# Second MLP: a norm queued behind the split of the operand lS2

## The chip, the cores and the metric

The kernel runs on one core of one Trainium2 chip. The metric is the device time of one execution, in microseconds (us), as a median over runs. Engines are named as the profile names them: PE is TensorE's matmul array and PEld its weight loads, DVE is VectorE, ACT is ScalarE, POOL is GpSimd, SP is SyncE, which issues the DMAs.

## What is computed

Linear attention, then a first MLP with a leaky activation, then a second MLP with a softmax-weighted unit and a layer norm. The change lies in the second MLP:

```python
def _moe2_ref(x, w_in, w_out, g_ln):
    h = x @ w_in                                   # 4608 x 512 by 512 x 1024
    h_max = np.max(h, axis=-1, keepdims=True)
    e = np.exp(h - h_max)
    sm = e / (np.sum(e, axis=-1, keepdims=True) + 1e-09)
    solu = h * sm
    mu = np.mean(solu, axis=-1, keepdims=True)
    var = np.mean((solu - mu) ** 2, axis=-1, keepdims=True)
    ln = (solu - mu) / np.sqrt(var + 1e-06) * g_ln
    return (ln @ w_out).astype(np.float32)         # 4608 x 1024 by 1024 x 512
```

## The kernel before

Every f32 operand of a matmul is held as a high part (the value as ACT copies it to fp32r) and a low part (what is left, by a DVE subtraction); `put` writes the two. A product is then three matmuls: high by high, high by low, low by high. Both matrix products of the second MLP are made in seven block products instead of eight, by sums and differences of quarter blocks (operands A11, A12, A22, S1 to S4 on the one side, B11, B21, B22, T1 to T4 on the other).

The rows are worked off in 18 *pairs* of 128-row tiles, z = 0 and z = 1. For pair n the steps are:

- `pe_h2(n, part)`: the first product on PE, 42 matmuls of 512 columns in two PSUM banks, h2a and h2x. ACT copies partial sums aside (r1, r2, r5, line 1411), since the next product goes on in the same bank; DVE and ACT add the halves into hs_n_0 and hs_n_1.
- `norm(n, z)`: softmax unit and layer norm of one tile. It is a chain over three engines: the maximum on DVE (line 1460), exp on ACT (1461), the sum's reciprocal and the product on DVE (1450 to 1453), square on ACT (1463), a power on POOL between two small DVE steps (1456, 1457, 1465), and the last line on ACT (1466), which writes the tile el that the next step transposes. Below, "exp", "square" and "last line" of z = 0 or z = 1 are these.
- `pe_tr(n, z)`: 8 transposes on PE into two PSUM tiles tp that are used in turn, and the operands of the second product. For z = 0 ACT copies fA11 and fA12 out and writes two high parts, DVE writes the two low parts. For z = 1 the order in the code is fA22, the sum s (1524), operand A22, the difference s3 (1527), S1, s once more (1529), S2, S3, f12 (1532), S4. The tiles are named lS1, lS2, lS3 for S1 to S3, and l1 for A22 and S4.
- `pe_out(n, part)`: the second product, 84 matmuls of 256 columns in the banks oa and ox (lines 1547 to 1549), with ACT copies or1, or2, or5 (1553) and DVE additions (1567, 1575, 1577). The third of its seven products, S2 by T2, is the first that needs lS2.

The loop over n (0 to 15) interleaves these: `pe_h2(n + 1, 0)`, `pe_tr(n, 0)`, `pe_h2(n + 1, 1)`, `pe_tr(n, 1)`, `norm(n + 1, 0)`, `pe_h2(n + 1, 2)`, loads, `pe_out(n, 0)`, `norm(n + 1, 1)`, `pe_out(n, 1)`. The code's order isn't the order on the engines. A scheduler that works before the program runs puts each engine's instructions in a row, by what it reckons to be ready; on the chip each engine takes its row strictly one after the other and waits where an operand isn't there. `tc.issue_after(ins)` tells that scheduler that whatever the block traces on the engine of `ins` comes behind `ins` in the row; it adds no wait on the chip. In the loop's early turns there is extra work: up to 14 `y_late` steps, each an ACT copy and a DVE subtraction of 256 columns into a single tile yl (its next use waits until the DMA of the last one has landed), some with a DVE addition of 128x2x128 ahead. The last pairs (`end`) are ordered by hand.

A *turn* below is one value of n in this loop.

Of the kernel before, what the change touches and what calls it, by code (L numbers as in the profile page):

```python
# [12 lines left out]
AF = mybir.ActivationFunctionType  # L13
ALU = mybir.AluOpType
# [6 lines left out]
def attention_then_two_mlps(  # L21
# [32 lines left out]
    V, S, G, T = nc.vector, nc.scalar, nc.gpsimd, nc.tensor  # L54
# [51 lines left out]
    def f32(ap):  # L106
        return ap.bitcast(F32)
# [22 lines left out]
        ]  # L130

    def put(hi, lo, src, eng=V):
        S.activation(hi, src, AF.Copy)  # L133
        eng.tensor_tensor(lo, src, f32(hi), ALU.subtract)  # L134


    wps = [tc.alloc_tile_pool(name="wp0", bufs=7 + FU, side="right")]
# [1241 lines left out]
    def load_y(n):  # L1379


        i, z = divmod(n, 2)
        ys[n] = {}
        for o in STAT:
            ys[n][o] = m2["pool"].tile([P, 2, 2, P], F32R, tag=f"y{o}", bufs=1, name=f"y_{n}_{o}")
            asked = nc.sync.dma_start(out=f32(ys[n][o]), in_=y_d[i][STAT.index(o)][:, z])
        return asked
# [4 lines left out]
    def pe_h2(n, part):  # L1392
        if part == 0:
            hb[n] = [psum["h2"].tile([P, N], F32, tag=f"h2{z}", name=f"h2{z}_{n}") for z in "ax"]
            hs[n] = [gp.tile([P, F2], F32, tag="t", name=f"hs_{n}_{z}") for z in range(2)]
        (ba, bx), (ha, hb2) = hb[n][:2], hs[n]
        op = ys[n]

        def prod(t, a, b, start):
            for z in range(2):  # L1400
                ah, al = op[a][:, 0, z, :], op[a][:, 1, z, :]
                bh, bl = wi[b, z][:, 0, :], wi[b, z][:, 1, :]
                go_on = dict(skip_group_check=not start)
                T.matmul(t, ah, bh, start=start and z == 0, stop=False, **go_on)  # L1404
                T.matmul(t, ah, bl, start=False, stop=False, **go_on)  # L1405
                at_end = T.matmul(t, al, bh, start=False, stop=z == 1, **go_on)  # L1406
            return at_end

        def hold(src, z):
            r = m2["pool"].tile([P, N], F32, tag="r", bufs=3, name=f"r{z}_{n}")  # L1410
            S.activation(r, src, AF.Copy)
            return r

        if part == 0:
            prod(ba, "A11", "B11", True)
            r1 = hold(ba, 1)
            prod(bx, "A12", "B21", True)
            V.tensor_tensor(ha[:, 0:N], bx, r1, ALU.add)
            prod(ba, "S2", "T2", False)
            hb[n].append(hold(ba, 2))  # L1420
            at_end = prod(bx, "S1", "T1", True)
            hb[n].append(hold(bx, 5))
            return at_end
        elif part == 1:
            prod(ba, "S3", "T3", False)
            V.tensor_tensor(hb2[:, N:F2], ba, hb[n][3], ALU.add)
            prod(bx, "S4", "B22", False)
            V.tensor_tensor(ha[:, N:F2], bx, hb[n][2], ALU.add)
        else:
            prod(ba, "A22", "T4", False)  # L1430
            S.activation(hb2[:, 0:N], ba, AF.Copy)
# [3 lines left out]
    def norm(n, z):  # L1435
        for piece in norm_pieces(n, z):
            piece()

    def norm_pieces(n, z):
        t = 2 * n + z  # L1440
        h = hs[n][z]
        st = m2["pool"].tile([P, 8], F32, tag="st", bufs=4, name=f"st_{t}")
        nm, se, rs, su, sq, rstd = (st[:, z:z + 1] for z in range(6))
        if t == 0:
            m2["pool"].tile([P, 3 * SHIFT], F32, name="l_edge")
        e = m2["pool"].tile([P, F2], F32, tag="el", bufs=2, name=f"el_{t}")
        lns[t] = e

        def solu():
            V.tensor_scalar_add(se, se, 1e-9)  # L1450
            V.reciprocal(rs, se)
            V.scalar_tensor_tensor(e, h, rs, e, ALU.mult, ALU.mult, accum_out=su)  # L1452
            V.tensor_scalar_mul(su, su, -1.0 / F2)

        def spread():
            V.tensor_scalar(sq, sq, 1.0 / F2, 1e-6, ALU.mult, ALU.add)
            G.tensor_tensor(rstd, sq, mhalf, ALU.pow)

        return [
            lambda: V.tensor_reduce(nm, h, AX.X, ALU.max, negate=True),  # L1460
            lambda: S.activation(e, h, AF.Exp, bias=nm, accum_out=se),
            solu,
            lambda: S.activation(h, e, AF.Square, bias=su, accum_out=sq),
            spread,
            lambda: V.tensor_tensor(su, su, rstd, ALU.mult),  # L1465
            lambda: S.activation(e, e, AF.Identity, bias=su, scale=rstd),  # L1466
        ]
# [3 lines left out]
    def lt_op(n, o):  # L1471
        free = {"A22": KEPT[0], "S4": KEPT[1], "S3": KEPT[2]}
        if n == NPR - 2 and o in free:
            b, z = free[o]
            del wi[b, z]
            t = w2p["pool"].tile([P, 2, 4, P], F32R, tag=f"{b}{z}", name=f"l{o}_{n}")
        elif o in ("S1", "S2", "S3"):
            t = m2["pool"].tile([P, 2, 4, P], F32R, tag=f"l{o}", name=f"l{o}_{n}")
        else:
            y, z = divmod(("A11", "A12", "S4", "A22").index(o), 2)  # L1480
            if (n, y) not in lts:
                lts[n, y] = pair_tile(y, f"l{y}_{n}")[:, 0:4 * N].rearrange("p (z s f q) -> p z s f q", z=2, s=2, f=4)
            t = lts[n, y][:, z]
        lts[n, o] = t
        return t

    def lt_put(n, o, src):
        t = lt_op(n, o)
        put(t[:, 0], t[:, 1], src)

    lf = {}

    def turned_rows(n, z):

        ln = lns.pop(2 * n + z)
        tps = []
        for g in range(2):
            tp = psum["o"].tile([P, 4, P], F32, tag="tp", bufs=2, name=f"tp_{n}_{z}_{g}")
            for f in range(4):
                c = (4 * g + f) * P  # L1500
                T.transpose(tp[:, f, :], ln[:, c:c + P], ident)  # L1501
            tps.append(tp)
        return tps

    def pe_tr(n, z):


        tps = turned_rows(n, z)

        def copy(o, src):  # L1510
            lf[n, o] = m2["pool"].tile([P, 4, P], F32, tag=f"f{o}", bufs=1, name=f"f{o}_{n}")
            S.activation(lf[n, o], src, AF.Copy)  # L1512

        if z == 0:
            copy("A11", tps[0])
            lt_put(n, "A11", tps[0])
            copy("A12", tps[1])
            lt_put(n, "A12", tps[1])
        else:
            copy("A22", tps[1])  # L1520
            f11, f12, f22 = (lf.pop((n, o)) for o in ("A11", "A12", "A22"))
            t = gp.tile([P, 2, N], F32, tag="rn", bufs=1, name=f"fs_{n}")
            s, s3 = (t[:, y, :].rearrange("p (f q) -> p f q", f=4) for y in range(2))
            V.tensor_tensor(s, tps[0], f22, ALU.add)
            a21 = tps[0]
            lt_put(n, "A22", tps[1])
            V.tensor_tensor(s3, f11, a21, ALU.subtract)
            lt_put(n, "S1", s)
            V.tensor_tensor(s, s, f11, ALU.subtract)
            lt_put(n, "S2", s)  # L1530
            lt_put(n, "S3", s3)
            V.tensor_tensor(f12, f12, s, ALU.subtract)
            lt_put(n, "S4", f12)
# [137 lines left out]
    def store_y(asked):  # L1671
        with tc.issue_after(asked.ins):
            while y_kept:
                y_kept.pop(0)()

    for n in range(NPR - 2):
        at_end = pe_h2(n + 1, 0)
        with ExitStack() as behind:
            if n == 0:
                behind.enter_context(tc.issue_after(at_end.ins))  # L1680
            pe_tr(n, 0)
        if n:
            store_y(asked)
        if n and y_late:
            y_late.pop(0)()
        pe_h2(n + 1, 1)
        pe_tr(n, 1)
        norm(n + 1, 0)
        pe_h2(n + 1, 2)
        asked = load_y(n + 2)  # L1690
        store_y(asked)
        pe_out(n, 0)
        norm(n + 1, 1)
        if n and y_late:
            y_late.pop(0)()
        if n < NPR - 3:
            pe_out(n, 1)
    m, n = NPR - 2, NPR - 1
# [5 lines left out]
    def end():  # L1704
# [9 lines left out]
        out_prod(m - 1, ba, "S3", "T3", False)  # L1714
        V.tensor_tensor(oy[:, W:C], ba, r5, ALU.add)
        pe_tr(m, 0)
        pe_h2(n, 1)
        top0, exp0, solu0, square0, spread0, mult0, line0 = norm_pieces(n, 0)
# [123 lines left out]
```

## Time and profile before

| what | value |
|---|---|
| median of 3 runs | 1282.57 us (1281.18 to 1283.31) |
| profiled execution, first to last instruction (span) | 1282.1 us |
| PE busy | 1243.1 us, 97% |
| PEld busy | 1111.6 us, 87% |
| DVE busy | 1009.0 us, 79% |
| ACT busy | 792.1 us, 62% |
| POOL busy | 27.0 us, 2% |

The profile is of one execution, with the start of each instruction from the span's beginning. A busy PE isn't a PE at its peak: its matmuls overlap one another and their ends are modelled. The second MLP's loop runs from about 895 to 1232 us, its hand-ordered end from there to 1282 us.

### The profile page before, as it was taken

How to read it: one execution, taken by the hardware profiler on the slowest of the kernel's cores; microseconds unless marked ns; L12 is line 12 of the kernel's file. 1: busy time of each engine (PE TensorE's matmuls, PEld its weight loads, DVE VectorE, ACT ScalarE, POOL GpSimd, SP SyncE). 2: the span in 40 equal slices, each digit the busy share in tenths (PEclk: the TensorE clock that was granted, in tenths of full speed). 3: DMA queues.
4: the chain of work that ended last, by engine and by line, in shares of the span. 5: the costliest groups of instructions: out<-in, count | busy, mean ns of one | idle time of the engine just before them, and what ended most of it. 6: DMA issues, size and time to landing. Idle time of an engine off the chain costs nothing.

```text
span 1282.1 us, 22034 instructions
## 1 busy us (share of the span) xinstructions
PE 1243.1 (97%) x8443; PEld 1111.6 (87%) x8443; DVE 1009.0 (79%) x1818; ACT 792.1 (62%) x1371; POOL 27.0 (2%) x52
## 2 busy tenths in 40 slices
PE   4899999999999999999999999999999999999998
PEld 3788898898988899998998999987888888898988
DVE  7899978988867876787889888864777778686865
ACT  5776554654655665564656655544777677777774
POOL 0100000000000000000000000000000000000000
PEclk9899999999999999999999999999999999999999
DMA  9954553454426510534666457579444335333312
GB/s 254 281 168 138 143 151 105 120 175 101 140 78 198 189 34 33 214 134 174 235 230 222 191 201 262 194 240 393 134 124 145 116 131 157 114 110 110 113 59 50
DMA packets 153401, 203.83 MB, mean 159 GB/s; under 512 B 57144, under 2 KB 105296, under 8 KB 150096
## 3 DMA queue, kind: packets, MB, share of 16 engines
q1 hardware_dynamic: 152208, 201.38, 48.7%
q0 software_dynamic: 1088, 1.05, 0.5%
q8 instruction: 66, 1.08, 0.4%
q14 instruction: 39, 0.32, 0.1%
HBM read 126.37 MB, written 76.02 MB: 158 GB/s over the span
## 4 chain that ended last, share of the span: by engine, by line
PE 75%; DVE 9%; DMA 8%; ACT 5%; issue 2%; SPq 1%; POOL 0%; ACTq 0%; DVEq 0%; POOLq 0%
PE acc L471 8%; PE acc L472 8%; PE acc L473 8%; PE ga L361 4%; PE ga L362 4%; PE ga L363 4%; PE gx L361 3%; PE gx L363 3%; PE gx L362 3%; PE oa L1547 2%; PE tp L1501 2%; PE h2a L1404 2%; PE h2a L1406 2%; PE h2a L1405 2%; PE oa L1549 2%; PE oa L1548 2%
## 5 line engine op out<-in xcount | busy, mean ns | idle before, releaser
L471 PE MATMUL acc<-gg,w 128*128 128x512 f32 x576 | 226.0, 392 | 1.4 <-ACT w L212 0.9
L472 PE MATMUL acc<-gg,w 128*128 128x512 f32 x576 | 226.9, 394 | 0.0
L473 PE MATMUL acc<-gg,w 128*128 128x512 f32 x576 | 224.2, 391 | 0.0
L473 PEld LDWEIGHTS acc<-gg,w 128*128 128x128 f32 x576 | 108.1, 188 | 23.1 <-DVE w L213 0.3
L471 PEld LDWEIGHTS acc<-gg,w 128*128 128x128 f32 x576 | 108.2, 188 | 20.9 <-ACT w L212 1.0
L472 PEld LDWEIGHTS acc<-gg,w 128*128 128x128 f32 x576 | 108.2, 188 | 17.9 <-DVE gg L134 0.3
L134 DVE TENSOR_TENSOR gg<-t,gg 128x1024 fp32r<-128x1024 f32 x72 | 87.9, 1220 | 15.3 <-ACT gg L133 15.2
L133 ACT ACTIVATE gg<-t 128x1024 fp32r<-128x1024 f32 x72 | 76.6, 1064 | 27.2 <-DVE t L452 20.0
L452 DVE SCALAR_TENSOR_TENSOR t<-rn,calpha,t 128x512 f32<-128x512 f32 x120 | 84.6, 746 | 8.2 <-ACT rn L449 8.1
L449 ACT ACTIVATE rn<-t 128x1024 f32<-128x1024 f32 x60 | 63.2, 1053 | 31.7 <-DVE t L438 31.5
L134 DVE TENSOR_TENSOR l<-tp,l 128x512 fp32r<-128x512 f32 x50 | 34.2, 684 | 46.5 <-ACT l L133 46.5
L361 PE MATMUL ga<-xT,w_S 128*128 128x256 f32 x240 | 68.2, 284 | 0.3 <-ACT r L370 0.2
L363 PE MATMUL ga<-xT,w_S 128*128 128x256 f32 x240 | 67.0, 279 | 0.0
L362 PE MATMUL ga<-xT,w_S 128*128 128x256 f32 x240 | 67.0, 279 | 0.0
L370 ACT ACTIVATE r<-ga 128x512 f32<-128x512 f32 x60 | 35.7, 596 | 42.4 <-PE ga L363 42.2
L1466 ACT ACTIVATE el<-el,st 128x1024 f32<-128x1024 f32 x36 | 44.5, 1242 | 20.9 <-DVE st L1465 10.0
L389 PE MATMUL h<-xB,w_c 128*128 128x256 f32 x192 | 55.1, 289 | 1.4 <-ACT w_c L212 1.3
L391 PE MATMUL h<-xB,w_c 128*128 128x256 f32 x192 | 55.1, 288 | 1.1 <-DVE w_c L213 1.0
L390 PE MATMUL h<-xB,w_c 128*128 128x256 f32 x192 | 54.7, 285 | 0.0
L1512 ACT ACTIVATE fA<-tp 128x512 f32<-128x512 f32 x50 | 30.2, 603 | 30.1 <-PE tp L1501 30.1
L361 PEld LDWEIGHTS ga<-xT,w_S 128*128 128x128 f32 x240 | 45.1, 188 | 2.7 <-ACT r L370 1.0
L1452 DVE SCALAR_TENSOR_TENSOR el<-hs,st,el 128x1024 f32<-128x1024 f32 x36 | 46.1, 1281 | 0.6
(408 smaller groups left out, 3994.2 us busy)
## 6 DMA issues: line engine op xcount, KB each, us to landing
y_S<-y_d SPq DMA_DIRECT2D x72, 256.0 KB, 3.0
xraw<-x_d SPq DMA_DIRECT2D x16, 1024.0 KB, 4.9
y_d<-yo_S SPq DMA_DIRECT2D x32, 512.0 KB, 3.2
y_A<-y_d SPq DMA_DIRECT2D x54, 256.0 KB, 2.7
y_d<-yo_A SPq DMA_DIRECT2D x24, 512.0 KB, 3.1
p_d<-pt SPq DMA_DIRECT2D x36, 256.0 KB, 3.2
part<-p_d SPq DMA_DIRECT2D x9, 1024.0 KB, 8.5
q<-in_q_dram SPq DMA_DIRECT2D x16, 512.0 KB, 5.6
```

The source lines that it names most:

```text
L133: S.activation(hi, src, AF.Copy)
L134: eng.tensor_tensor(lo, src, f32(hi), ALU.subtract)
L361: T.matmul(bank[:, z, :], wh, x[:, 0, c, :], start=first and z == 0, stop=False, **go_on)
L362: T.matmul(bank[:, z, :], wh, x[:, 1, c, :], start=False, stop=False, **go_on)
L363: T.matmul(bank[:, z, :], wl, x[:, 0, c, :], start=False, stop=c == 1, **go_on)
L389: T.matmul(out, w[:, 0, c, :], x[:, 0, c % 2, :], start=c == 0 and h == 0, stop=False, **go_on)
L391: T.matmul(out, w[:, 1, c, :], x[:, 0, c % 2, :], start=False, stop=c == KC - 1, **go_on)
L449: S.activation(rn, t, AF.Relu, scale=-1.0)
L452: V.scalar_tensor_tensor(t[:, j, :], rn[:, j, :], calpha[:, fg + j:fg + j + 1], t[:, j, :], ALU.mult, ALU.add)
L471: T.matmul(a, wh, g[:, 0, :], start=u == 0 and f == 0, stop=False)
L472: T.matmul(a, wh, g[:, 1, :], start=False, stop=False)
L473: T.matmul(a, wl, g[:, 0, :], start=False, stop=u == NU - 1 and f == FU - 1)
```

## The change

`put` and `lt_put` return the two instructions they make, `pe_tr` keeps those of S2, and the loop traces `norm(n + 1, 1)` in a block that queues it behind both: its ACT instructions behind the high part of lS2 of pair n, its DVE instructions behind the low part.

```diff
     def put(hi, lo, src, eng=V):
-        S.activation(hi, src, AF.Copy)
-        eng.tensor_tensor(lo, src, f32(hi), ALU.subtract)
+
+        return S.activation(hi, src, AF.Copy), eng.tensor_tensor(lo, src, f32(hi), ALU.subtract)
...
         t = lt_op(n, o)
-        put(t[:, 0], t[:, 1], src)
-
-    lf = {}
+        return put(t[:, 0], t[:, 1], src)
+
+    lf, split_at = {}, {}
...
-            lt_put(n, "S2", s)
+            split_at[n] = lt_put(n, "S2", s)
...
         pe_out(n, 0)
-        norm(n + 1, 1)
+        with ExitStack() as behind:
+            for ins in split_at.pop(n):
+                behind.enter_context(tc.issue_after(ins.ins))
+            norm(n + 1, 1)
```

No instruction is added or taken away; the rows on the engines change. On ACT in turn 9, from behind or1_9 on (el_20 and el_21, st_20 and st_21 are norm(10, 0) and norm(10, 1); lS2_9, l1_9 are operands of pair 9; r1_11, r2_11 belong to pe_h2(11)), before:

```order
L1461 ACTIVATE el_21_12125,st_21_12124<-hs_10_1_11935,st_21_12124 128x1024
L133 ACTIVATE lS2_9_12022<-fs_9_12012 128x512
L1411 ACTIVATE r1_11_12188<-h2a_11_12178 128x512
L133 ACTIVATE l1_9_12014<-fA12_9_11982 128x512
L1553 ACTIVATE or2_9_12108<-oa_9_12065 128x256
L1463 ACTIVATE hs_10_0_11934,st_20_12031<-el_20_12032,st_20_12031 128x1024
L1553 ACTIVATE or5_9_12122<-ox_9_12066 128x256
L1466 ACTIVATE el_20_12032<-el_20_12032,st_20_12031 128x1024
L1463 ACTIVATE hs_10_1_11935,st_21_12124<-el_21_12125,st_21_12124 128x1024
L1580 ACTIVATE ob1_9_12068<-oa_9_12065 128x256
L1466 ACTIVATE el_21_12125<-el_21_12125,st_21_12124 128x1024
L1411 ACTIVATE r2_11_12203<-h2a_11_12178 128x512
```

The same place on ACT after the change:

```order
L134 ACTIVATE lS2_9_12022<-fs_9_12012 128x512
L134 ACTIVATE l1_9_12014<-fA12_9_11982 128x512
L1411 ACTIVATE r1_11_12188<-h2a_11_12178 128x512
L1553 ACTIVATE or2_9_12108<-oa_9_12065 128x256
L1553 ACTIVATE or5_9_12122<-ox_9_12066 128x256
L1461 ACTIVATE el_21_12125,st_21_12124<-hs_10_1_11935,st_21_12124 128x1024
L1463 ACTIVATE hs_10_0_11934,st_20_12031<-el_20_12032,st_20_12031 128x1024
L1466 ACTIVATE el_20_12032<-el_20_12032,st_20_12031 128x1024
L1463 ACTIVATE hs_10_1_11935,st_21_12124<-el_21_12125,st_21_12124 128x1024
L1580 ACTIVATE ob1_9_12068<-oa_9_12065 128x256
L1411 ACTIVATE r2_11_12203<-h2a_11_12178 128x512
L1466 ACTIVATE el_21_12125<-el_21_12125,st_21_12124 128x1024
```

The exp of z = 1 moves from the head of the piece to behind or5, five rows on; r2 moves from behind the last line of z = 1 to ahead of it.

On DVE in turn 9, from behind the low part of lS1_9 and the first small step of norm(10, 0), before:

```order
L1460 TENSOR_REDUCE st_21_12124<-hs_10_1_11935 128x1
L1529 TENSOR_TENSOR fs_9_12012<-fs_9_12012,fA11_9_11977 128x512
L134 TENSOR_TENSOR lS3_9_12025<-fs_9_12012,lS3_9_12025 128x512
L1532 TENSOR_TENSOR fA12_9_11982<-fA12_9_11982,fs_9_12012 128x512
L1451 RECIPROCAL st_20_12031<-st_20_12031 128x1
L1567 TENSOR_TENSOR ob0_9_12067<-ox_9_12066,or1_9_12081 128x256
L134 TENSOR_TENSOR lS2_9_12022<-fs_9_12012,lS2_9_12022 128x512
L1452 SCALAR_TENSOR_TENSOR el_20_12032,st_20_12031<-hs_10_0_11934,st_20_12031,el_20_12032 128x1024
L134 TENSOR_TENSOR l1_9_12014<-fA12_9_11982,l1_9_12014 128x512
L1453 TENSOR_SCALAR st_20_12031<-st_20_12031 128x1
L1450 TENSOR_SCALAR st_21_12124<-st_21_12124 128x1
L1451 RECIPROCAL st_21_12124<-st_21_12124 128x1
```

The same place on DVE after the change:

```order
L1529 TENSOR_TENSOR fs_9_12012<-fs_9_12012,fA11_9_11977 128x512
L134 TENSOR_TENSOR lS3_9_12025<-fs_9_12012,lS3_9_12025 128x512
L1532 TENSOR_TENSOR fA12_9_11982<-fA12_9_11982,fs_9_12012 128x512
L134 TENSOR_TENSOR lS2_9_12022<-fs_9_12012,lS2_9_12022 128x512
L1451 RECIPROCAL st_20_12031<-st_20_12031 128x1
L1567 TENSOR_TENSOR ob0_9_12067<-ox_9_12066,or1_9_12081 128x256
L134 TENSOR_TENSOR l1_9_12014<-fA12_9_11982,l1_9_12014 128x512
L1452 SCALAR_TENSOR_TENSOR el_20_12032,st_20_12031<-hs_10_0_11934,st_20_12031,el_20_12032 128x1024
L1460 TENSOR_REDUCE st_21_12124<-hs_10_1_11935 128x1
L1453 TENSOR_SCALAR st_20_12031<-st_20_12031 128x1
L1575 TENSOR_TENSOR ob1_9_12068<-oa_9_12065,or5_9_12122 128x256
L1450 TENSOR_SCALAR st_21_12124<-st_21_12124 128x1
```

The maximum of z = 1 moves behind the product of z = 0, eight rows on; the low part of lS2 moves ahead of line 1451 and line 1567.

Turns 0 to 2, 4, 5, 7 to 9, 11 to 13 and 15 have this order, with yl copies between in turns 1 to 7. In turns 3, 6, 10 and 14 the rows on ACT stand in another order. In turn 10 before the change, behind or1_10 (el_22 and el_23 are norm(11, 0) and norm(11, 1)):

```order
L1461 ACTIVATE el_23_12371,st_23_12370<-hs_11_1_12181,st_23_12370 128x1024
L133 ACTIVATE lS2_10_12268<-fs_10_12258 128x512
L1411 ACTIVATE r1_12_12434<-h2a_12_12424 128x512
L133 ACTIVATE l1_10_12260<-fA12_10_12228 128x512
L1553 ACTIVATE or2_10_12354<-oa_10_12311 128x256
L1463 ACTIVATE hs_11_0_12180,st_22_12277<-el_22_12278,st_22_12277 128x1024
L1553 ACTIVATE or5_10_12368<-ox_10_12312 128x256
L1466 ACTIVATE el_22_12278<-el_22_12278,st_22_12277 128x1024
L1463 ACTIVATE hs_11_1_12181,st_23_12370<-el_23_12371,st_23_12370 128x1024
```

The same place on ACT after the change:

```order
L134 ACTIVATE lS2_10_12268<-fs_10_12258 128x512
L1411 ACTIVATE r1_12_12434<-h2a_12_12424 128x512
L134 ACTIVATE l1_10_12260<-fA12_10_12228 128x512
L1463 ACTIVATE hs_11_0_12180,st_22_12277<-el_22_12278,st_22_12277 128x1024
L1553 ACTIVATE or2_10_12354<-oa_10_12311 128x256
L1461 ACTIVATE el_23_12371,st_23_12370<-hs_11_1_12181,st_23_12370 128x1024
L1466 ACTIVATE el_22_12278<-el_22_12278,st_22_12277 128x1024
L1553 ACTIVATE or5_10_12368<-ox_10_12312 128x256
L1411 ACTIVATE r2_12_12449<-h2a_12_12424 128x512
L1463 ACTIVATE hs_11_1_12181,st_23_12370<-el_23_12371,st_23_12370 128x1024
```

Here the square of z = 0 stands ahead of the exp of z = 1 and the last line of z = 0 right behind it; on DVE the product of z = 0 stands ahead of the low part of lS2 in these turns. On PE the first matmuls with lS2 move up by several matmuls of 512 columns in most turns (by six in turn 9), and in most turns one matmul of the following product comes to stand between the two groups of transposes of z = 1.

## Rows read from the trace of the kernel before

**Rows 1.** Stretches: length, busy us (and instructions) of PE, PEld, DVE, ACT, POOL; PEclk; DMA share; GB/s.

```profile
1098.00:1120.00 22.00, 22.00 (x146) 19.74 (x145) 16.12 (x34) 16.07 (x31) 1.09 (x2) 1.00 0.35 116
995.00:997.20 2.20, 0.37 (x2) 0.00 (x0) 0.52 (x3) 1.80 (x4) 0.00 (x0) 1.00 0.72 199
997.20:1001.00 3.80, 3.48 (x16) 3.49 (x17) 3.47 (x9) 1.26 (x3) 0.00 (x0) 0.55 0.06 22
```

**Rows 2.** Waits, 895 to 1240 us: who waited for whom, total us, times, longest.

```profile
PEld oa L1547 <- ACT lS L133: 10.4, 16, 2.6
PE oa L1547 <- ACT lS L133: 4.3, 7, 2.1
```

**Rows 3.** Timeline of DVE, turn 9: start, length, instruction, [idle before].

```profile
1101.79 0.68 DVE L1524 TENSOR_TENSOR fs<-tp,fA 128x512 f32<-128x512 f32 x1
...
1104.38 1.21 DVE L1460 TENSOR_REDUCE st<-hs 128x1 f32<-128x1024 f32 x1
1105.51 0.68 DVE L1529 TENSOR_TENSOR fs<-fs,fA 128x512 f32<-128x512 f32 x1
...
1107.70 0.68 DVE L134 TENSOR_TENSOR lS<-fs,lS 128x512 fp32r<-128x512 f32 x1
1108.30 1.28 DVE L1452 SCALAR_TENSOR_TENSOR el<-hs,st,el 128x1024 f32<-128x1024 f32 x1
...
1110.18 0.14 DVE L1450 TENSOR_SCALAR st<-st 128x1 f32<-128x1 f32 x1
...
1110.55 1.29 DVE L1452 SCALAR_TENSOR_TENSOR el<-hs,st,el 128x1024 f32<-128x1024 f32 x1
...
1111.76 0.15 DVE L1456 TENSOR_SCALAR st<-st 128x1 f32<-128x1 f32 x1
...
1112.57 0.16 DVE L1465 TENSOR_TENSOR st<-st 128x1 f32<-128x1 f32 x1
...
1123.26 0.68 DVE L1524 TENSOR_TENSOR fs<-tp,fA 128x512 f32<-128x512 f32 x1
```

**Rows 4.** Timeline of ACT, turn 9.

```profile
1105.62 1.15 ACT L1461 ACTIVATE el<-hs,st 128x1024 f32<-128x1024 f32 x1 [0.67 <-DVE st L1460]
1106.68 0.18 ACT L1461 ACTIVATION_READ_ACCUMULATOR el<-hs,st 128x1 f32 x1
1106.77 0.61 ACT L133 ACTIVATE lS<-fs 128x512 fp32r<-128x512 f32 x1
...
1112.83 1.25 ACT L1466 ACTIVATE el<-el,st 128x1024 f32<-128x1024 f32 x1 [1.03 <-DVE st L1453]
1113.98 1.13 ACT L1463 ACTIVATE hs<-el,st 128x1024 f32<-128x1024 f32 x1
...
1116.31 1.25 ACT L1466 ACTIVATE el<-el,st 128x1024 f32<-128x1024 f32 x1 [0.83 <-DVE st L1465]
1117.46 0.57 ACT L1411 ACTIVATE r<-h2a 128x512 f32<-128x512 f32 x1
...
1118.41 0.60 ACT L1512 ACTIVATE fA<-tp 128x512 f32<-128x512 f32 x1
```

**Rows 5.** Timeline of DVE: line 1524 in turns 0, 4, 5, 8 and 15.

```profile
901.26 0.68 DVE L1524 TENSOR_TENSOR fs<-tp,fA 128x512 f32<-128x512 f32 x1
...
989.47 0.68 DVE L1524 TENSOR_TENSOR fs<-tp,fA 128x512 f32<-128x512 f32 x1
...
1014.63 0.68 DVE L1524 TENSOR_TENSOR fs<-tp,fA 128x512 f32<-128x512 f32 x1
...
1080.27 0.68 DVE L1524 TENSOR_TENSOR fs<-tp,fA 128x512 f32<-128x512 f32 x1
...
1230.82 0.68 DVE L1524 TENSOR_TENSOR fs<-tp,fA 128x512 f32<-128x512 f32 x1
```

**Rows 6.** Timeline of ACT: the yl copy of turn 4, and two rows of the end.

```profile
995.40 0.42 ACT L133 ACTIVATE yl_A<-part 128x256 fp32r<-128x256 f32 x1 [2.71 <-DMA y_d<-yl_S]
...
1245.33 1.24 ACT L1466 ACTIVATE el<-el,st 128x1024 f32<-128x1024 f32 x1 [0.62 <-DVE st L1465]
1246.48 0.58 ACT L1512 ACTIVATE fA<-tp 128x512 f32<-128x512 f32 x1
```

## The prediction, made before the changed kernel ran

> **What bounds the kernel now.** The change touches only the second MLP's loop, so I first read that stretch by windows. From 1098 to 1120 us PE is busy 22.00 of 22.00 us at a granted clock of 1.00 [rows 1], while DVE and ACT are busy about 16 each. Read alone, this says that PE bounds the turn and that nothing on ACT or DVE matters. The waits say a little more: the first matmul with lS2 (line 1547) waits for ACT's high part of lS, 16 times, 10.4 us counted on the weight loads and 4.3 us counted on the matmul array [rows 2], so once in each turn.
>
> Then the timelines of ACT and DVE over one turn, followed as a loop. A turn's beat is line 1524 on DVE, 1101.79 us in turn 9 and 1123.26 us in turn 10: 21.47 us [rows 3]. I write times as offsets from 1101.79. DVE runs without a gap from 0 to 9.97: the maximum of z = 1 at 2.59, line 1529 at 3.72, the low part of lS2 at 5.91, the product of z = 0 at 6.51, that of z = 1 at 8.76, line 1456 of z = 0 at 9.97, line 1465 at 10.78 [rows 3]. From there the chain goes on in ACT's row: last line of z = 0 at 11.04, square of z = 1 at 12.19, last line of z = 1 at 14.52, r2 at 15.67, r5, and fA11 at 16.62 [rows 4]; the copies behind fA11 feed DVE, which is at line 1524 again at 21.47, 4.85 us after fA11. So DVE, POOL and ACT alone make **a closed loop of 21.47 us in a turn, as long as PE's own turn**. Averages hide it, since each of these engines is idle for a part of it. Over turns 8 to 14 the beat is (1230.82 - 1080.27) / 7 = 21.51 us, over turns 0 to 7 (1080.27 - 901.26) / 8 = 22.38 us, with one of 1014.63 - 989.47 = 25.16 us in turn 4 [rows 5].
>
> **The change, part by part.** It adds and removes no instruction, so the cost is what the new rows do to this loop, walked with the same durations.
>
> *lS2 comes earlier.* With the maximum of z = 1 out of the way, line 1529 starts at 2.59 in place of 3.72. Its length of 0.68 later, at about 3.3, the high part can start, where it stood at 4.98 (1106.77) [rows 4]. PE's row asks for it earlier too (six matmuls of 512 columns in turn 9), so most of the wait in [rows 2] should go, but not surely all. This alone is worth nothing in a turn if the loop over ACT and DVE doesn't become shorter.
>
> *The norm of z = 1 comes later.* DVE after the change: line 1529 at 2.59, then lS3, line 1532 and the low part of lS2 at steps of 0.60 (1107.70 to 1108.30 [rows 3]): lS2 at 4.39. Lines 1451 and 1567 take 0.39 (before, line 1529 plus three such steps ends at 5.52 and lS2 starts at 5.91), l1 starts at 5.38, the product of z = 0 at 5.98, and 1.21 later (1110.55 to 1111.76 [rows 3]) the maximum of z = 1 at 7.19, where it was 2.59. The exp follows 1.24 after the start of the maximum (1104.38 to 1105.62 [rows 3, 4]): at 8.43, where it was 3.83. Its sum is there 1.24 later (1105.62 to 1106.86 [rows 4]), at 9.67, and now DVE has nothing left to fill that time but line 1575. Lines 1450 and 1451 take 0.37 (1110.18 to 1110.55 [rows 3]), the product of z = 1 starts at 10.08 with 0.04 for the handover, and line 1456 of z = 0, which stands behind it, at 11.29 in place of 9.97: **1.32 us later**.
>
> *The rest of the loop* keeps its steps: line 1465 0.81 later at 12.10, last line of z = 0 at 12.36, square of z = 1 at 13.51, last line of z = 1 2.33 behind that (1113.98 to 1116.31 [rows 4]) at 15.84. Here r2 now stands ahead of that line and gives back one copy of 0.48 (half of 1117.46 to 1118.41 [rows 4]): r5 at 16.99, fA11 at 17.47 in place of 16.62. The loop becomes 22.32 us, **0.85 longer**. PE can't hide this: it waits for r5 and for the low parts of l0 that free the tp banks, so the stall moves from lS2 to the transposes.
>
> *The four other turns* (3, 6, 10, 14) have the square of z = 0 ahead of the exp and the last line of z = 0 right behind it. The same walk for turn 10 puts fA11 at about 16.3, shorter than before, so there PE's own turn counts: 21.51 less the wait at lS2 that goes, 0 to 10.4 / 16 = 0.65 [rows 2]. I take 0.1, since in turns 8 to 14 loop and PE are nearly equal.
>
> *Turns 8 to 14*, then: five long ones, 5 x (22.32 - 21.51) = +4.05, and two of the other kind, -0.2: **+3.85**.
>
> *Turns 0 to 7* took 179.01 us. After: turns 0, 1, 7 at 22.32; 2 and 5 at 22.8 (their 128x2x128 additions come where DVE waits for the exp; I take 0.5 for what doesn't fit, bounds 0 and 1.2, one product's length [rows 3]); 3 and 6 at 21.5; turn 4 at 23.1. In turn 4 the yl copy waited for a landing until 995.40 and started at 995.40 - 989.47 = 5.93 [rows 5, 6]. It stood ahead of the exp and lS2, and PE was busy 0.37 of 2.20 us; behind that the clock was 0.55 for 3.80 us, near the lower of its two levels, which cost about 3.80 x 0.45 = 1.7 us [rows 1]. After the change lS2 stands ahead of it, so both go; but l1's copy stands behind it, due at about 4.5, which delays the product of z = 0 by 0 (the DMA lands as in its neighbours) to 1.7. I take the middle. The sum is 66.96 + 45.6 + 43.0 + 23.1 = 178.7: **-0.3**, bounds -3.5 and +2.5.
>
> *The end.* In turn 15 the first copy of the end (fA11) starts at 1246.48, as soon as ACT is through with the last line of z = 1 at 1245.33 [rows 6]. Here r2 stood ahead of that line already, so nothing is given back: 0 to +1.32; I take **+1.3**, since the copy starts the moment that line lets it.
>
> Sum: 3.85 - 0.3 + 1.3 = +4.85 us. The profiled span of 1282.1 lies 0.5 below the median of 1282.57, and what lies around the span is untouched: 1282.57 + 4.85 = 1287.4.
>
> **The rivals.** *The waits go and nothing takes their place: faster.* For it: the last line of z = 1 ends at 1117.56 [rows 4], and the code has the transposes of z = 0 and 12 matmuls of pe_h2 ahead of those that need it, so seen from PE the norm has time to spare. Price: between PE's 4.3 and PEld's 10.4 us of [rows 2], plus the 1.7 of clock: 6.0 to 12.1; the matmul array's own count is nearer to what is lost, so about 1276. It decides if fA11 and r5 don't wait for the norm's last line. Against it: ACT takes its row in order, and r5 and fA11 stand behind that line in the new rows too. This is what a rule of the Trainium skill would give. Its page Perfetto Trace Analysis, section Optimization Strategy, says to find the gaps on the engine that one optimises for, see what it waits for, and make that start sooner; this change does just that for the gap of [rows 2]. The rows agree that the gap is there; whether closing it pays they leave to the loop behind it.
>
> *The early turns pay for the late ones: no change.* If turn 4 falls from 25.16 to 22.32 whole and the additions of turns 2 and 5 fit, the first eight turns give 2 x 0.5 + 0.8 more, and the end may take half of its 1.3: 4.85 - 1.8 - 0.65 = +2.4, 1285.0; with loop steps 0.2 shorter in five turns, 1284.0. For it: turn 4's landing is out of line with its neighbours and may not come again. Against: five of the seven late turns have nothing to gain there.
>
> *Turn 4's kind of stall spreads.* If the new PE waits bring the clock down as in [rows 1], each costs up to 1.7 us more; three would give 1292.5. Against: that fall came behind some 2 us without work, and the new waits are parts of 0.85.
>
> **How the numbers follow.** About 0.2%, 2.6 us, is what a measurement of this kernel can tell from no change. My forecast, slower at about 1287, has a chance of 0.58, the spread stall 0.03 more. No change has 0.25: the early turns' gain, or a loop that isn't quite as tight as I walk it. Faster has 0.14. The range of 1280 to 1291.5 leaves out most of the faster case, the spread stall, and the worst ends of turn 4 and of the additions. I round to 1287.
>
> **What would show it.** In the profile after: line 1524's beat at about 22.3 in turns 8, 9, 11, 12, 13 and about 21.4 in 10 and 14; the exp of z = 1 some 8.4 behind line 1524; no wait of line 1547 for lS; new waits at the transposes of z = 1 or at line 1404 for r5; no fall of the clock in turn 4. I am wrong if the beat of the late turns stays at 21.5 or less (then fA11 isn't bound to the norm's last line), or if turns 0 to 7 give back 3 us or more.

## The result, and the profile after

The changed kernel takes 1291.99 us (median of 5 runs, 1291.16 to 1293.52), the kernel before 1283.01 beside it: **slower, by a ratio of 1.0068 [1.0056, 1.0080]**, +7.2 to +10.3 us. The forecast was 1287.0, in a range of 1280 to 1291.5. The direction and, in the late turns, the mechanism were right; the size was not, about half of what came.

Line 1524 starts a turn on DVE, so its 16 starts split the span into four pieces. I use this split for every run below; the pieces are differences of those starts, and the last one reaches to the last instruction. The first piece, ahead of the loop's first line 1524, isn't in the tables: it took 900.0 to 901.3 us in the four profiled executions of before that there are by now, and 899.1 to 905.9 in the others, so that totals of single executions differ by more than the turns do. After has two profiled executions, every other kernel one.

| us | turns 0 to 7 | turns 8 to 14 | from line 1524 of turn 15 on |
|---|---|---|---|
| before, first trace [rows 5] | 179.01 | 150.55 | 51.3 |
| before, three more | 176.49, 177.97, 177.01 | 150.56, 150.55, 150.47 | 51.2, 51.2, 51.2 |
| after, two traces | 180.43, 180.28 | 155.51, 155.64 | 53.0, 52.7 |
| difference of the means | +2.7 | +5.0 | +1.6 |
| the prediction's term | -0.3 | +3.85 | +1.3 |

These three pieces sum to +9.4, inside the measured interval.

First the windows of after: length, busy us (and instructions) of PE, PEld, DVE, ACT, POOL; the granted clock; DMA share; GB/s. The first is turn 12, the other two are a place in turn 15 that the prediction didn't have.

```profile
1170.42:1192.86 22.44, 22.20 (x144) 19.30 (x143) 15.68 (x34) 15.80 (x29) 1.10 (x2) 1.00 0.36 106
1246.74:1249.02 2.28, 0.39 (x3) 0.00 (x1) 2.15 (x6) 1.46 (x3) 0.55 (x1) 1.00 0.00 0
1249.02:1253.02 4.00, 4.00 (x15) 3.46 (x16) 0.54 (x4) 3.18 (x5) 0.55 (x1) 0.57 0.00 0
```

Turn 12 is 22.44 us long and PE is busy in 22.20 of them: PE still looks full, as in [rows 1], while the turn has become 0.9 us longer. DVE and ACT are busy in 15.7 and 15.8 of them, where it was 16.1 of 22.00.

The waits of after, 895 to 1240 us (who waited for whom: total us, times, longest), answer [rows 2]. `put` is at line 134 in place of 133.

```profile
PEld tp L1501 <- issue: 6.6, 12, 0.8
PEld oa L1547 <- ACT lS L134: 4.6, 11, 0.9
PEld tp L1501 <- DVE l L134: 3.9, 9, 0.5
...
PE tp L1501 <- DVE l L134: 3.6, 11, 0.6
...
PE oa L1547 <- ACT lS L134: 0.6, 1, 0.6
```

The wait at lS2 fell from 10.4 to 4.6 us on PEld and from 4.3 to 0.6 on PE. In its place stand waits of the transposes (line 1501), a good part of them for the low parts of l, which free their banks. Whoever reads only the first of these two sentences would call the change a success. And most of the wait at lS2 never lay in the late turns, where the change costs most. The same wait from 1080 to 1240 us (turns 8 to 15), before and after:

```profile
PEld oa L1547 <- ACT lS L133: 2.8, 8, 0.5
...
PEld oa L1547 <- ACT lS L134: 1.9, 5, 0.4
```

The timeline of DVE in turn 12 answers [rows 3] (start, length, instruction, [idle before]):

```profile
1170.42 0.68 DVE L1524 TENSOR_TENSOR fs<-tp,fA 128x512 f32<-128x512 f32 x1
...
1173.06 0.69 DVE L1529 TENSOR_TENSOR fs<-fs,fA 128x512 f32<-128x512 f32 x1
...
1174.88 0.68 DVE L134 TENSOR_TENSOR lS<-fs,lS 128x512 fp32r<-128x512 f32 x1
...
1177.68 1.21 DVE L1460 TENSOR_REDUCE st<-hs 128x1 f32<-128x1024 f32 x1
1178.81 0.14 DVE L1453 TENSOR_SCALAR st<-st 128x1 f32<-128x1 f32 x1
1180.00 0.42 DVE L1575 TENSOR_TENSOR ob<-oa,or 128x256 f32<-128x256 f32 x1 [1.04 <-issue]
1180.34 0.14 DVE L1450 TENSOR_SCALAR st<-st 128x1 f32<-128x1 f32 x1
...
1180.72 1.29 DVE L1452 SCALAR_TENSOR_TENSOR el<-hs,st,el 128x1024 f32<-128x1024 f32 x1
...
1182.74 0.16 DVE L1465 TENSOR_TENSOR st<-st 128x1 f32<-128x1 f32 x1 [0.33 <-POOL st L1457]
...
1192.86 0.68 DVE L1524 TENSOR_TENSOR fs<-tp,fA 128x512 f32<-128x512 f32 x1
```

and that of ACT [rows 4]:

```profile
1173.79 0.63 ACT L134 ACTIVATE lS<-fs 128x512 fp32r<-128x512 f32 x1 [0.21 <-DVE fs L1529]
...
1178.98 1.15 ACT L1461 ACTIVATE el<-hs,st 128x1024 f32<-128x1024 f32 x1
...
1182.99 1.25 ACT L1466 ACTIVATE el<-el,st 128x1024 f32<-128x1024 f32 x1 [1.63 <-DVE st L1453]
1184.14 1.14 ACT L1463 ACTIVATE hs<-el,st 128x1024 f32<-128x1024 f32 x1
...
1186.48 1.24 ACT L1466 ACTIVATE el<-el,st 128x1024 f32<-128x1024 f32 x1 [0.36 <-DVE st L1465]
1187.62 0.58 ACT L1411 ACTIVATE r<-h2x 128x512 f32<-128x512 f32 x1
1188.10 0.59 ACT L1512 ACTIVATE fA<-tp 128x512 f32<-128x512 f32 x1
```

The maximum of z = 1 stands 7.26 behind line 1524 (it was 2.59), the exp 8.56, the product of z = 1 10.30, the last line of z = 1 16.06, fA11 17.68 (it was 16.62), the next line 1524 22.44. What the page of the profile shows of this is next to nothing: PE 97% busy before and after, DVE 79% and 78%, ACT 62% twice.

### The profile page after: what moved, and what is told of

Read it like the earlier page. It is cut to its first block, busy times and chain, and to the rows that moved or that the text cites. A ratio compares the mean times of both kernels' runs of the same rounds, so it can differ in the third digit from the quotient of the medians.

```text
span 1289.8 us, 22041 instructions
## 1 busy us (share of the span) xinstructions
PE 1247.0 (97%) x8443; PEld 1107.0 (86%) x8443; DVE 1009.5 (78%) x1818; ACT 796.4 (62%) x1371; POOL 27.2 (2%) x52
## 4 chain that ended last, share of the span: by engine, by line
PE 73%; DVE 11%; ACT 6%; DMA 6%; issue 2%; POOL 1%; SPq 0%; ACTq 0%; DVEq 0%; POOLq 0%
PE acc L471 9%; PE acc L472 9%; PE acc L473 9%; PE ga L361 4%; PE ga L363 4%; PE ga L362 4%; PE gx L361 3%; PE gx L363 3%; PE gx L362 3%; PE oa L1547 2%; PE oa L1549 2%; PE oa L1548 2%; PE h L391 2%; PE h L389 1%; PE h L390 1%
## 5 line engine op out<-in xcount | busy, mean ns | idle before, releaser
L134 ACT ACTIVATE gg<-t 128x1024 fp32r<-128x1024 f32 x72 | 76.6, 1064 | 30.7 <-DVE t L452 23.1
```

What stands on the lines that cost most here:

```text
L134: return S.activation(hi, src, AF.Copy), eng.tensor_tensor(lo, src, f32(hi), ALU.subtract)
```

## The experiments

Every ratio is against the kernel before, run on the same chip at the same time.

| kernel | ratio [95%] | turns 0 to 7 | 8 to 14 | from turn 15 on |
|---|---|---|---|---|
| DVE's edge alone | 1.0081 [1.0069, 1.0093] | 180.24 | 155.37 | 53.0 |
| ACT's edge alone | 0.9993 [0.9982, 1.0003] | 175.10 | 151.44 | 51.2 |
| turns 0 to 7 alone | 1.0024 [1.0016, 1.0033] | 180.20 | 150.52 | 51.2 |
| turns 8 to 15 alone | 1.0034 [1.0022, 1.0047] | 177.31 | 156.18 | 50.3 |
| after, half a last line | 1.0054 [1.0034, 1.0074] | 178.99 | 153.98 | 53.0 |
| before, half a last line | 0.9991 [0.9977, 1.0005] | 175.88 | 150.42 | 50.8 |
| after, last line moved | 1.0013 [0.9999, 1.0028] | 176.45 | 152.32 | 51.4 |
| before, last line moved | 1.0026 [1.0012, 1.0040] | 178.52 | 151.87 | 51.4 |
| after, but turn 15 | 1.0059 [1.0042, 1.0076] | 180.82 | 155.33 | 51.2 |
| after, but turn 0 | 1.0065 [1.0046, 1.0084] | 179.18 | 155.08 | 52.7 |
| ACT's edge, turns 0 to 7 | 0.9991 [0.9979, 1.0004] | 175.17 | 150.32 | 51.3 |
| before, less PE work | 0.9971 [0.9956, 0.9986] | 173.64 | 149.78 | 51.3 |

### Which of the two edges, and in which turns

The change queues the norm behind two instructions: the high part of lS2 on ACT and the low part on DVE. Each alone:

```diff
-            for ins in split_at.pop(n):
+            for ins in split_at.pop(n)[1:]:   # DVE's edge alone; [:1] for ACT's
```

> The change with its edge on VectorE alone: the norm of z = 1 is queued behind the low part of lS2, but not behind its high part on ScalarE. Theory (the loop over DVE, POOL and ACT is made longer because the maximum of z = 1 goes behind the low part of lS2): this edge alone is the whole change, so the time lies 7 to 10 us above before, as after's +8.98, with the exp of z = 1 at about 8.5 behind line 1524 in turn 12. Rival (ACT's edge, which puts the exp behind the high part, is what costs): under 3 us above before, with the exp at about 4 to 5.

> The change with its edge on ScalarE alone: the exp of z = 1 stands behind the high part of lS2, the maximum of z = 1 stays where it was on DVE (ahead of line 1529). Theory (the place of the maximum on DVE is what costs): the exp comes about 0.5 later, at 4.9 in place of 3.83 behind line 1524, its sum is there at about 6.2, well ahead of the product of z = 1 at 8.76, so the loop stays at 21.5: 0 to -4 us against before (the wait at line 1547 falls from 10.4 us to a half, and turn 4's stall may go), beat in turn 12 21.4 to 21.6. Rival (ACT's edge costs): +5 to +9, with the last line of z = 1 ending later than 15.8 behind line 1524.

DVE's edge alone puts the rows of every engine in the same order as the whole change; it has its time, +0.81%, and its pieces. ACT's edge alone is no slower than before. So what costs is the place of the maximum on DVE, not that of the exp behind lS2's high part on ACT. The waits of ACT's edge alone, 895 to 1235 us:

```profile
PEld oa L1547 <- ACT lS L134: 6.2, 16, 1.2
```

It takes 4.2 of the 10.4 us of this wait, where the whole change takes 5.8, and leaves the maximum early: in its one trace turns 0 to 7 fall to 175.1, below every execution of before, and turns 8 to 14 rise by 0.9, to beats of 21.6. In the total that isn't told apart from nothing.

The change in a part of the turns:

```diff
-            for ins in split_at.pop(n):
+            for ins in split_at.pop(n)[:2 if n < 8 else 0]:   # n >= 8 for the other
```

> The change in turns 0 to 7 alone, later turns as before. Theory (each turn pays by its own loop; the two traces differ by +1.4 in turns 0 to 7, by +5.0 in turns 8 to 14 and by +1.75 behind them): +1 to +3 us against before, with turn 4 at about 23.3 in place of 25.2 and turns 8 to 14 at 21.5 each. Rival (what the early turns do decides the beat of all that follow, through the store and the loads of y that were begun there): +6 to +9, with turns 8 to 14 at 22.2.

> The change in turns 8 to 15 alone, turns 0 to 7 as before. Theory: turns 8 to 14 and the end pay here too, +5 to +8 us against before, with turns 0 to 7 at 179.0 in sum as before and long turns at 22.4. Rival (the early turns decide): under 2 us.

Each half pays for itself: with the early turns changed, the late ones have 21.5 each, and the other way round 22.4 (six long ones: turns 10 and 14 took the long order, turn 11 the short one). So next to nothing is carried from the early turns into the late; the exception is turn 9, 22.47 here and 22.88 in after. But the early half costs 2.1 to 4.2 us, where the first two traces had shown 1.4, and the late half less than its turns, since its end is shorter than before's. ACT's row there, turn 15:

```profile
1246.55 0.60 ACT L1512 ACTIVATE fA<-tp 128x512 f32<-128x512 f32 x1
1247.04 0.59 ACT L134 ACTIVATE l<-tp 128x512 fp32r<-128x512 f32 x1
1247.60 1.25 ACT L1466 ACTIVATE el<-el,st 128x1024 f32<-128x1024 f32 x1
```

Its line 1524 is at 1233.00, so fA11 comes 13.55 behind it, and the last line of z = 1 stands behind two copies. In before fA11 came 15.66 behind line 1524 and in after 17.34. This order fell out of the scheduler by chance, and it points at the instruction that holds fA11. It doesn't settle the matter: the same row of DVE has line 1418 ahead of the product of z = 1, 8.89 behind line 1524 in place of 11.50 in after, and PE doesn't stand for it there as it does in after (shown below, with the ends of the loop).

### Is it the loop? The last line made shorter, and moved

The prediction's loop goes through the last line of z = 1, r5 and fA11 in ACT's row. If the loop sets the beat of the long turns, a shorter last line shortens them by as much; if the new row of PE does, it changes nothing.

```diff
-            lambda: S.activation(e, e, AF.Identity, bias=su, scale=rstd),
+            lambda: S.activation(e[:, 0:cols], e[:, 0:cols], AF.Identity, bias=su, scale=rstd),
```

> The changed kernel with the last line of z = 1 run over 512 of its 1024 columns in every turn (the other half of that tile stays without its scale and shift). In long turns r5, fA11 and the three copies behind it stand behind this instruction on ACT. A 512-column ACT instruction starts the next 0.48 later, the 1024-column last line 1.14 (1186.48 to 1187.62 in turn 12), so about 0.6 goes. Theory (the loop over DVE, POOL and ACT sets the beat of long turns): their beat falls from 22.44 to about 21.8, turns 3, 6, 10 and 14 stay at 21.4 to 21.6, in all about 12 x 0.6 = -7 us against after: +1 to +4 against before. Rival (the new PE row with its gaps at the transposes sets the beat): beat unchanged at 22.4, +8 to +10 against before.

> The kernel before with the last line of z = 1 run over 512 of its 1024 columns in every turn (the rest without its scale and shift); 0.6 less in the same loop. Theory of the prediction (the loop of 21.47 and PE's own turn are nearly equal before): the beat in turns 8 to 14 falls by 0 to 0.15, since PE has 22.00 of 22.00 us busy there; 0 to -3 us in all. Rival (the loop alone sets the beat before as well, PE has room): beat 20.9, -7 to -9 us.

ACT in turn 12 of the changed kernel with half a last line:

```profile
1183.69 0.82 ACT L1466 ACTIVATE el<-el,st 128x512 f32<-128x512 f32 x1 [0.35 <-DVE st L1465]
1184.42 0.58 ACT L1411 ACTIVATE r<-h2x 128x512 f32<-128x512 f32 x1
1184.89 0.59 ACT L1512 ACTIVATE fA<-tp 128x512 f32<-128x512 f32 x1
```

From the last line to r5 it is 0.73 in place of 1.14: 0.41 less. The beat of the long turns fell from 22.44 to 21.98: 0.46 less. I had expected 0.6, by the spacing of other instructions of 512 columns; what the instruction gave back is what the turn gave back. In the total less came of it, +0.54% [0.34, 0.74], not told apart from the +0.68% of the change, because the rows of turns 3, 6, 10 and 14 took the long order too and went from 21.5 to 22.0. In the kernel before the same cut leaves the beat of turns 8 to 14 at 21.45 to 21.56. So the loop sets the beat after, and before there is something else as long.

Then the last line kept whole and taken out of the loop's way:

```diff
+        with tc.issue_after(copied[n].ins):
+            while line_of:
+                line_of.pop(0)()
...
-            norm(n + 1, 1)
+            *first, line = norm_pieces(n + 1, 1)
+            for piece in first:
+                piece()
...
+        if n < NPR - 3:
+            line_of.append(line)
```

`copied[n]` is the fourth copy of turn n on ACT, the high part of A12.

> The changed kernel with the last line of z = 1 taken from its place ahead of r5 and fA11 in ACT's row and put behind the four copies of the next turn (fA11, l0, fA12, l0); the rows around it shift a little with it (the square of z = 0 ahead of the exp of z = 1 in every turn). Theory: fA11 no longer waits for this line, so the four copies come 1.1 earlier and the transposes of z = 1 wait for the line instead: the beat of turns 8 to 14 falls to PE's own turn, 21.4 to 21.6; 0 to +3 us against before. Rival (the PE row sets the beat): 22.4 stays.

> The kernel before with only that move: the last line of z = 1 behind the four copies of the next turn. Theory: the loop of before becomes shorter by up to 1.1, PE's own turn stays; so the beat of turns 8 to 14 falls by 0 to 0.15, and early turns, where DVE has more to do, may gain up to 0.5 each: 0 to -5 us. Rival (transposes of z = 1 wait longer for their operand, which comes 1.9 later): +2 to +8.

On top of the change it takes the beat to 21.7 or 21.8 in all of turns 2 to 14, the long ones down from 22.4, the four others up from between 21.4 and 21.6, and most of the cost with it: +0.13% [-0.01, +0.28]. The long turns don't come down to 21.5, and since the rows about it shifted as well it is the weaker of the two tests. On top of before the rival was right: 21.7 in place of 21.5, +0.26%. There PE's weight loads wait for the last line at the transposes in each of turns 8 to 14, 2.3 us in all, which they didn't before:

```profile
PEld tp L1501 <- ACT el L1466: 2.3, 7, 0.4
```

### What set the beat before

Four matmuls of each turn left out, the low part of l by the high part in the product with lS3, with all rows else in the order of before in turns 8 to 14:

```diff
-            T.matmul(t, l[:, 0, f, :], bl, start=False, stop=False, **go_on)
-            T.matmul(t, l[:, 1, f, :], bh, start=False, stop=f == 3, **go_on)
+            short = a == "S3" and n < NPR - 3
+            T.matmul(t, l[:, 0, f, :], bl, start=False, stop=short and f == 3, **go_on)
+            if not short:
+                T.matmul(t, l[:, 1, f, :], bh, start=False, stop=f == 3, **go_on)
```

> The kernel before without four of the 128x256 matmuls of each turn (the l times h part of the product with lS3, left out in turns 0 to 14); 4 x 0.1165 = 0.47 us of PE's work in a turn. Theory of the prediction (loop over DVE, POOL and ACT as long as PE's own turn): the beat of turns 8 to 14 stays near 21.5 (21.4 to 21.5), since the loop holds it. Rival (only PE sets the beat before, the loop has room): 21.03, -7 us in all.

```profile
1163.74:1185.12 21.38, 21.36 (x139) 18.82 (x138) 15.56 (x34) 15.53 (x29) 1.10 (x2) 1.00 0.39 112
```

Turn 12 in the windows, from line 1524 to line 1524: the beat is 21.38 or 21.39 in six of turns 8 to 14, 0.1 below before, where PE has 0.47 less to do. What it no longer does, it waits: from 1080 to 1235 us its weight loads have two waits, at the transposes and for ACT's r, that before has not (there the wait at lS2 is the only one).

```profile
PEld tp L1501 <- issue: 1.6, 7, 0.2
PEld h2a L1404 <- ACT r L1411: 1.2, 7, 0.2
```

Take the two tests together: 0.4 off the loop leaves 21.5, 0.47 off PE gives 21.39. **Before, PE's turn and the loop were within about 0.1 us of each other**, as the prediction read them, and whichever is made longer is paid in full. In turns 0 to 7 the sum is 173.6 in place of 176.5 to 179.0; at least 1.5 of that lies in turn 4 (21.49 in place of 23.01 or more), which varies from one execution to the next, so what PE's work counts for there isn't shown.

### The ends of the loop: turn 0 and turn 15

```diff
-            for ins in split_at.pop(n):
+            for ins in split_at.pop(n)[:0 if n >= NPR - 3 else 2]:   # [:2 if n else 0] for turn 0
```

> The change in turns 0 to 14, turn 15 as before. Theory (in turn 15 the maximum and the exp of z = 1 come 4.9 later behind line 1524, DVE's product of z = 1 holds back line 1418 for which PE waits 2.1 us, and the clock then falls to 0.59 for 4 us): from line 1524 of turn 15 to the last instruction 51.2 to 51.4 us as before in place of 53.0; turns 0 to 14 as after. -1.5 to -2 us against after, +7 to +8.5 against before. Rival (the end is late only because turn 14 hands it over late): 53.0 stays.

> The change in turns 1 to 15, turn 0 as before. Theory (in turn 0 r2 and r5 stand between the copies fA11, l0, fA12 of ACT's row in the changed kernel, which a long turn's 22.44 doesn't have): turn 0 falls from 23.40 to 22.2, the others stay: -1.2 us against after, +7 to +9 against before. Rival (the turn's own state at the loop's start, whatever the row): 23.4 stays.

Both fall as expected in the trace: 51.2 in place of 53.0 behind line 1524 of turn 15, and turn 0 at 22.20 in place of 23.40. In the total neither is told apart from after. What the rows of turn 15 of after show, PE first:

```profile
1246.51 0.39 PE L1405 MATMUL h2a<-wi_T,y_S 128*128 128x512 f32 x1
1246.74 0.39 PE L1406 MATMUL h2a<-wi_T,y_S 128*128 128x512 f32 x1
1249.02 0.50 PE L1404 MATMUL h2x<-wi_T,y_S 128*128 128x512 f32 x1 [1.90 <-DVE hs L1418]
...
1250.09 0.63 PE L1404 MATMUL h2x<-wi_T,y_S 128*128 128x512 f32 x1
1250.51 0.63 PE L1405 MATMUL h2x<-wi_T,y_S 128*128 128x512 f32 x1
```

the same place in before:

```profile
1240.78 0.40 PE L1406 MATMUL h2a<-wi_T,y_S 128*128 128x512 f32 x1
1241.59 0.50 PE L1404 MATMUL h2x<-wi_T,y_S 128*128 128x512 f32 x1 [0.42 <-DVE hs L1418]
```

and DVE of after:

```profile
1247.01 1.28 DVE L1452 SCALAR_TENSOR_TENSOR el<-hs,st,el 128x1024 f32<-128x1024 f32 x1
...
1248.28 0.68 DVE L1418 TENSOR_TENSOR hs<-h2x,r 128x512 f32<-128x512 f32 x1
```

Line 1418, which reads the bank h2x, is queued behind the product of z = 1, and that product is late. PE stands for 2.05 us beyond its usual spacing; in before it stood there for 0.58. So the late norm holds PE in a second place, beside the last line that holds fA11. That this stall lengthens the end by itself isn't shown: fA11 comes 1.68 later behind line 1524 (17.34 against 15.66), and the piece is 1.4 us longer where the clock stayed at 1.00 behind the stall (52.7), 1.8 where it fell (53.0).

Turn 0 fell as I had expected, but not for the reason that I had written down, the two r copies between the copies of the transposes. Its rows in after, first ACT:

```profile
914.56 1.14 ACT L1463 ACTIVATE hs<-el,st 128x1024 f32<-128x1024 f32 x1
...
915.96 0.58 ACT L1411 ACTIVATE r<-h2a 128x512 f32<-128x512 f32 x1
...
923.25 0.60 ACT L1512 ACTIVATE fA<-tp 128x512 f32<-128x512 f32 x1 [2.20 <-PE tp L1501]
```

then PE:

```profile
916.59 0.50 PE L1404 MATMUL h2a<-wi_T,y_S 128*128 128x512 f32 x1 [0.79 <-ACT r L1411]
```

and the same ACT copy, fA22, in the changed kernel with the last line moved:

```profile
928.34 0.60 ACT L1512 ACTIVATE fA<-tp 128x512 f32<-128x512 f32 x1 [2.66 <-PE tp L1501]
```

In that kernel the four copies of turn 0 stand together and are through 2.5 us earlier, yet fA22 starts 22.41 behind line 1524 as in after, and the turn takes 23.40 as in after. With half a last line the turn is no shorter either (23.44). So neither the last line nor the r copies set the length of this turn. r1 does fit: in this turn it stands behind the late square of z = 1, 15.12 behind line 1524, where it is at 5.11 in turn 12. PE waits 0.79 for it, and from there to the transposes that fA22 needs it works without a gap. That was read from the rows, not tested by itself.

### ACT's edge in the early turns alone

```diff
+            for ins in split_at.pop(n)[:1 if n < 8 else 0]:
```

> The kernel before with the ScalarE edge alone, in turns 0 to 7 alone. With that edge in all turns, turns 0 to 7 took 175.1 (before 179.0) and turns 8 to 14 151.4 (before 150.55). Theory (each turn pays and gains by itself): 175.1 and 150.5, -2 us against before, 0.9 below the edge in all turns. Rival (the early turns of before take 177 to 178 in most executions, and 179.0 was a high one): about 0 to -1.5 against before.

The pieces are those expected, 175.2 and 150.3, but the time isn't told apart from that of before, nor from the same edge in all turns. No kernel here that computes the whole is shown to beat the kernel before.

### The same two kernels once more

> The kernel before once more, unchanged, for its turns 0 to 7. Theory: turn 4's 25.17 of the first trace was a late landing that most executions don't have: turn 4 at 22.4 to 23.2 and turns 0 to 7 at 177 to 177.6, so the change costs the early turns 2.5 to 3.5 us and not the 1.4 of the first two traces. Rival (that landing is late each time): turn 4 at 25 and turns 0 to 7 at 179.

> The kernel before once more, unchanged: as the run ahead of it, theory 177 to 177.6 for turns 0 to 7, rival 179.

> The kernel before once more, unchanged: as the two runs ahead of it, theory 177 to 177.6 for turns 0 to 7, rival 179; turns 8 to 14 at 150.5 and the end at 51.3 in each.

> The changed kernel once more, unchanged. Theory: turns 0 to 7 at 180.2 to 180.8 again (turn 4 at 23.2), turns 8 to 14 at 155.1 to 155.5, the end 53.0: it repeats, so the difference to the kernel before is set by what turn 4 does there. Rival: turn 4 moves by a microsecond or more here as well.

Before's turn 4 took 23.01, 23.83 and 23.05 us, where the first trace had 25.17; turns 0 to 7 averaged 177.2 in these three. After repeats within 0.15 in turns 0 to 7. The second of the three, the windows of the stall at lS2 and behind it:

```profile
993.82:996.02 2.20, 0.48 (x3) 0.05 (x1) 0.56 (x3) 1.57 (x4) 0.00 (x0) 1.00 0.61 208
996.02:999.82 3.80, 3.26 (x28) 3.26 (x28) 3.24 (x9) 2.04 (x5) 0.00 (x0) 1.00 0.05 18
```

The stall is there, as deep as in [rows 1], but the clock stayed at 1.00 behind it. In the other two the stall is 1.7 us, the clock 1.00. So the first trace held a turn 4 that the other three didn't have: its 25.17 is 1.9 above their mean. Three kernels that leave turn 4 in the order of before took 22.96 (turns 8 to 15 alone), 23.09 (half a last line) and 23.91 (last line moved). By the two executions with the same stall, 25.17 and 23.83, the clock fall was worth about 1.3, where the prediction has 1.7.

## Why the prediction was right in kind and wrong in size

**What bounds the kernel: right.** That the loop over DVE, POOL and ACT is as long as PE's turn was read from two timelines, against a windows view that says PE is full. The half last line and the left-out matmuls bear it out, to about 0.1 us.

**The maximum of z = 1 behind lS2: right.** The walk said 7.19, 8.43, 10.08, 15.84 and 17.47 for the maximum, the exp, the product, the last line and fA11; turn 12 has 7.26, 8.56, 10.30, 16.06 and 17.68. The turn was put at 22.32 and is 22.44.

**Turns 8 to 14: +3.85 forecast, +5.0 measured.** A small error of the walk five times, about 0.12 each, of which a part is line 1575: it stands ahead of line 1450 in DVE's row and started only at 1180.00, behind PE's last matmul into oa at 1179.62; so line 1450 started at 1180.34, while the exp's sum was there at 1180.22. I had counted it as a filler of idle time. The rest is turn 9, 22.88 in both traces of after, where line 1575 starts 0.73 us after the start of that matmul, in place of 0.38; the profile names the exp of z = 1 (line 1461) as what ended its wait. With turn 0 left as before, and with all early turns left so, turn 9 took 22.47, so it hangs on something of the turns ahead; why line 1575 waits longer there isn't settled. Turns 10 and 14 came at 21.4 to 21.5, as forecast.

**Turns 0 to 7: -0.3 forecast, +2.7 measured. This is the step that failed**, with 3.0 of the 4.5 us that are missing. It failed in two places. The baseline was one execution: 179.01, of which 25.17 was a turn 4 with a clock fall that three more executions didn't have; by the mean of the four it is 177.6, 1.4 lower. I took what the change would give back there from a row that was true once. And the changed turns take 180.4 where 178.7 was forecast: 1.1 of it in turn 0, where I took the long turn's 22.32 without walking that turn's own rows (r1 stands behind the late square there, and PE waits for it), 0.8 in turns 1 and 7, whose reason is open; turns 2 and 5 came 0.25 each below their 22.8. Turn 4 of after, 23.28 and 23.23, is close to the 23.1 forecast. The price of the wait had the same fault: I spread the 10.4 us at lS2 over 16 turns, 0.65 each, while 2.6 of it stood in that one turn 4 and 2.8 in all of turns 8 to 15. That the change in turns 0 to 7 alone costs +2.1 to +4.2 us agrees with the mean of the four, not with the first trace.

**The end: +1.3 forecast, +1.6 measured.** Right in size. fA11 comes 1.68 later, as the last line holds it. I had not followed line 1418 behind the late product, where PE stands 1.5 us longer than before; beyond the clock that fell behind it in one of the two executions (53.0 against 52.7), no cost of that stall is shown.

**The rivals.** That the waits go and nothing takes their place was wrong in its condition: r5 and fA11 do stand behind the last line. The rule of the Trainium skill that I had set beside it (Perfetto Trace Analysis, section Optimization Strategy) would have one close the gap on the engine that one optimises for. The trace disagrees in this case: the gap at lS2 went from 10.4 to 4.6 us, gaps at the transposes opened in its place, and the kernel became 0.7% slower. ACT's edge alone closes 4 us of the same gap; turns 8 to 14 become 0.1 longer each, and in the total neither a cost nor a gain is shown. The spread clock fall decided nothing: turns 8 to 14 hold the granted clock at 1.00.

**What was said to show it.** A beat near 22.3 in the long turns, 21.4 in 10 and 14, the exp at 8.4, waits at the transposes, no clock fall in turn 4: all came. "No wait of line 1547" did not: 4.6 us of it stayed.

## What to carry to other kernels

When one engine is busy nearly all the time, follow the others as a loop from turn to turn before moving work on them: a chain through three engines that are each idle for a part of the turn can be as long as the busy engine's turn, and then delaying one link is paid in full although the wait that one aimed at goes. Leave a maximum that feeds a chain of five steps where it is early: the other edge, ACT's, took 4 us off the same wait at no cost that could be measured, though at no gain either. When a test comes out as expected, look whether its reason did too: turn 0 came back to 22.20 for another reason than the one written down. And before a term of a sum is taken from one odd turn of a trace, ask whether that turn is the same in another execution: here one odd turn made 1.4 us of the error.

## What the runs showed of the hardware

A stall of PE of the same length brings the granted clock down in some executions and not in others. In before's turn 4 a stall of 2.31 us beyond the usual spacing (no matmul starts between 994.98 and 997.52) was followed by 0.55 for 3.8 us [rows 1], one of 2.42 us in another execution (993.91 to 996.56) by 1.00. In turn 15 of after a stall of 2.05 us was followed by 0.57 for 4 us, and in the second execution of the same kernel the same 2.05 us by 1.00:

```profile
1248.44:1250.74 2.30, 0.44 (x2) 0.01 (x1) 2.20 (x6) 1.51 (x3) 0.55 (x1) 1.00 0.00 0
1250.74:1254.74 4.00, 3.98 (x27) 3.70 (x28) 0.86 (x5) 3.08 (x5) 0.55 (x2) 1.00 0.01 4
```

At 0.57, near the lower of the two levels (1.2 GHz), matmuls of 512 columns start 0.42 us apart (1250.09 to 1250.51), ahead of the stall 0.23 (1246.51 to 1246.74). The same stall of turn 15 stands in three more traces: with DVE's edge alone and with half a last line 0.57 follows, with turn 0 left as before 1.00. What decides it isn't shown here; for a prediction it means that a stall's price has two values, 53.0 or 52.7 for the end in these five traces.
